# Loads of x in chunks of ten tokens paced by transposes, with masks built first, in a fused convolution and expert kernel

## Chip, core and metric

The kernel runs on one NeuronCore of a Trainium2 chip. The metric is the device time of one execution in microseconds; the time before is the median of three runs.

## What is computed

Inputs are `x` (8 batches x 4160 tokens x 192 channels, float32), `weight_gen` (8 x 4160 x 8 heads x 7 taps) and the weights of a small expert network. First a dynamic convolution: every token has its own softmax over seven taps per head, and the output is the weighted sum of the token and its six predecessors. Then a mixture of depths: a gate scores every output row, the 128 highest rows of each batch go through two matrix products, and the result, scaled by a sigmoid of the score, is added to these rows.

```python
w = softmax(weight_gen, axis=-1)                       # (B, S, H, K)
out = einsum('bshk,bskhg->bshg', w, windows(x, K))     # causal, zero padded, K = 7
scores = einsum('bsd,d->bs', out, w_gate)
for b in range(B):
    top = argpartition(-scores[b], 128)[:128]
    y = maximum(out[b, top] @ w1, 0) @ w2              # 192 -> 1024 -> 192
    out[b, top] += sigmoid(scores[b, top])[:, None] * y
```

## The kernel before

The 33,280 rows are laid on 128 partitions of 260 consecutive tokens each (`SP = 260`). `phase()` (L584) holds all the work of interest. Its main loop (L873) makes 65 passes, `NSUB = 65`, each for four tokens of every partition (`C = 4`). The code is under `manual_schedule`, so each engine executes its instructions in the order in which the program writes them; only dependencies make an engine wait.

`x` lives in a ring `xr` of 168 tokens (`RING`) and six of padding, in float16. `load_x(a, b)` (L599) brings in tokens a to b of all partitions; it is issued on POOL's queue and converts from float32. A slot of the ring can be overwritten once the products and transposes that read it are done.

In one pass of the loop:

- VectorE multiplies a window of x by the weights: `products` (L769, instruction at L781), into one of three `prod` buffers.
- TensorE adds the seven taps of the pass before with 28 small matmuls: `tap_sums` (L785, L791), into `cps`. ScalarE copies that out to `co` (L799), one of three buffers, and SP's queue stores it in two halves (L801).
- ScalarE and TensorE do the softmax of later weights in pieces of four passes: `exps` (L627, L630), `sums` (L644), `scaled` (L648). Weight pieces come by `load_wg` (L613) on SP's queue, three pieces ahead. `dup_weights` (L759) doubles a piece for the products.
- `dots()` (L674) computes each token's dot products with the gate. Its work is cut into groups of eight 128-wide transposes of x (L711), 5.33 tokens, that ScalarE copies to `xT` (L715) and TensorE multiplies by `gmat` (L696). `DOTS = 0.66` lets 1.32 groups run in each pass, so the dots run ahead of the products. A few passes later `score()` (L719) turns them into scores, and when all are known the selection and the expert passes follow.

Loads of x follow three rules. Tokens 0 to 12 are loaded at the start. The thirteen chunks between the entries of `edges` (L835: 12, 24, 34, 44, 54, 64, 76, 90, 104, 118, 132, 146, 160, 168) are each tied to the exponentials of weight piece 1 to 13 (L636 to L643): POOL issues the load once that ScalarE instruction has run. The tokens after 168 come in chunks of 20 at passes worked out in `late` (L860), without such a tie.

`gate_matrix()` (L111) and `selection_masks()` (L125) are small selects and ramps on POOL. The first needs `wcol`, four tiny loads by `load_gate()` (L104) on SP's queue. `expert_weights()` (L176) clears two tiles and loads `w1` and `w2` from POOL. The order of the start of `phase()` is written out in L817 to L858.

Of the kernel before, what the change touches and what calls it, by code (L numbers as in the profile page):

```python
# [20 lines left out]
def kernel(  # L21
# [10 lines left out]
    nc = tc.nc  # L32
    B, S, D = x.shape
# [4 lines left out]
    PAD = K - 1  # L38
    P = 128
    N = B * S  # L40
    SP = N // P
# [3 lines left out]
    RING = 168  # L45
    C = 4
# [5 lines left out]
    RUN = 128  # L52
    GRP = 8
# [530 lines left out]
    def phase():  # L584
# [23 lines left out]

        pieces = [(0, 1), (1, 3), (3, 5)] + [(a, a + 4) for a in range(5, NSUB, 4)]
# [17 lines left out]
        def exps(n):  # L627
            m = pieces[n][1] - pieces[n][0]
            es[n] = ep.tile([P, m, K, CH], FP16, tag="e", name="e")
            begun = nc.scalar.activation(  # L630
                out=es[n][:, :, :, :],
                in_=wgts[n].rearrange("p (s c) h k -> p s k (c h)", c=C), func=AF.Exp
            )
            if n + 3 < NP:
                load_wg(n + 3)
            if n in paced:  # L636
                tc.add_manual_dep(
                    load_x(*paced[n]).ins, begun.ins.name,
                    mybir.DependencyInfo(
                        mybir.DependencyClass.Sync, mybir.DependencyReason.DATA  # L640
                    ), reason="x chunks follow the weight pieces",
                )
# [31 lines left out]
        def dots():  # L674
# [7 lines left out]
            for i in range(len(plan) + 2):  # L682
# [20 lines left out]
                if i < len(plan):  # L703
# [11 lines left out]
                    nc.scalar.copy(out=xT[:, 0:m, :], in_=tps[:, 0:m, :])  # L715
                    xTs[i] = xT
                yield
# [100 lines left out]
        load_wg(0)  # L818
        make_identity(nc, identity[:])
# [13 lines left out]
        load_gate()  # L833
        load_wg(2)
        edges = [12, 24, 34, 44, 54, 64, 76, 90, 104, 118, 132, 146, 160, RING]  # L835
        paced = dict(enumerate(zip(edges[:-1], edges[1:]), 1))
# [19 lines left out]
        gate_matrix()  # L856
        selection_masks()
        sm = softmax()  # L858

        late = []  # L860
        for a in range(RING, SP, 20):
            b = min(SP, a + 20)
            free = (b - RING + PAD - 1) // C + 1
            late.append((max(free, int((a + PAD) / (2 * DOTS * RUN * GRP / D)) - 4), a, b))
# [8 lines left out]
        for g in range(NSUB + 1):  # L873
# [34 lines left out]
            if late and g >= late[0][0]:  # L908
                load_x(*late.pop(0)[1:])
            if g == 10:  # L910
                selection_constants()
            if g == 34:
                expert_weights()
# [9 lines left out]
    DOTS = 0.66  # L923
    with ExitStack() as cctx:
        with tc.manual_schedule():
            phase()
# [84 lines left out]
```

## Time and profile before

| what | value |
|---|---|
| time, median of 3 runs | 327.6 us (327.27 to 327.63) |
| the profiled execution | 326.92 us |
| its span in the profile | 325.2 us |
| VectorE (DVE) busy | 249.1 us, 77% |
| TensorE (PE) busy | 195.0 us, 60% |
| ScalarE (ACT) busy | 188.7 us, 58% |
| GpSimd (POOL) busy | 59.3 us, 18% |
| mean DMA rate | 158 GB/s |

The profile is of one execution, taken by the hardware profiler; its times count from the span's start. The busy shares are means over stages that differ: loading and convolving at first, then the end of the convolution beside the selection, then the expert passes. Queues are named after the engine that issues: SPq, POOLq. "Idle before, releaser" names what ended an engine's wait; a wait for several things is put down to the last.

### The profile page before, as it was taken

Reading aid. Unit: us, or ns where it says so; the run is one execution under the profiler, and the core shown is the slowest. Engines: PE = TensorE matmul, PEld = TensorE weight load, DVE = VectorE, ACT = ScalarE, POOL = GpSimd, SP = SyncE. Lnnn points to the kernel's source line nnn. Section 1 sums busy time; section 2 is a strip of 40 time slices with the busy share of each in tenths; the row PEclk is TensorE's granted clock in tenths of the full one; section 3 lists DMA queues with packets and bytes.
Section 4 is the critical chain, followed back from the end, with each engine's and each line's share of the span. In section 5 each row is a group of like instructions: output and inputs, shape, how many; then the busy total and the mean of one; then the engine's idle time right before and its main releaser. Section 6 shows DMA issues by size and latency. Waiting matters only on the chain.

```text
span 325.2 us, 7474 instructions
## 1 busy us (share of the span) xinstructions
PE 195.0 (60%) x3177; PEld 124.2 (38%) x3177; DVE 249.1 (77%) x249; ACT 188.7 (58%) x282; POOL 59.3 (18%) x81
## 2 busy tenths in 40 slices
PE   0287569796979150979887563133735777678300
PEld 0255336464647030656554222011513444455200
DVE  3789559999999380499999999999997778884000
ACT  4699299999999224799975512001432657555200
POOL 2880000000030400000000000000327852000180
PEclk9999559979997875699998965555585799999855
DMA  7959989999989999545563543011377986333320
GB/s 165 296 174 227 273 220 235 248 243 263 261 236 225 232 233 271 120 120 143 152 149 97 147 108 88 1 48 48 73 171 128 188 166 132 100 73 93 83 80 21
DMA packets 28080, 51.48 MB, mean 158 GB/s; under 512 B 4805, under 2 KB 22219, under 8 KB 28042
## 3 DMA queue, kind: packets, MB, share of 16 engines
q1 hardware_dynamic: 21962, 33.62, 35.1%
q0 software_dynamic: 6080, 17.34, 29.5%
q8 instruction: 26, 0.43, 0.5%
q14 instruction: 12, 0.10, 0.1%
HBM read 41.60 MB, written 26.35 MB: 209 GB/s over the span
## 4 chain that ended last, share of the span: by engine, by line
DVE 31%; PE 22%; ACT 16%; DMA 16%; issue 9%; POOL 3%; SPq 1%; POOLq 0%; ACTq 0%; DVEq 0%
DVE prod L781 20%; DMA out_dram<-co 13%; PE cps L791 10%; ACT e L630 4%; ACT co L799 4%; PE tps L711 4%; ACT xT L715 2%; POOL out_dram L417 2%; PE den L189 2%; PE yps L696 2%; ACT wd L762 2%; DMA wg_t<-in_weight_gen_dram 2%; DVE above L492 1%; PE sps L740 1%; DVE cnt L498 1%
## 5 line engine op out<-in xcount | busy, mean ns | idle before, releaser
L781 DVE TENSOR_TENSOR prod<-xr,wd 128x5376 f16<-128x5376 f16 (+1 forms) x84 | 192.3, 2315 | 5.7 <-PE cps L791 3.2
L791 PE MATMUL cps<-prod,ident 64*64 64x384 f16 x1820 | 112.7, 378 | 11.3 <-DVE prod L781 10.6
L799 ACT COPY co<-cps 128x768 f32<-128x768 f32 x65 | 52.6, 809 | 66.3 <-PE cps L791 33.6
L791 PEld LDWEIGHTS <-ident 64*64 64x64 f16 x1820 | 50.4, 119 | 63.5 <-issue 26.8
L715 ACT COPY xT<-tps 128x1024 f16<-128x1024 f16 (+1 forms) x50 | 50.7, 1022 | 5.3 <-PE tps L711 5.0
L249 POOL DMA_INDIRECT wsel<-in_weight_gen_dram,row_i x8 | 11.7, 1462 | 124.2 <-DVE win_i L217 122.0
L711 PE MATMUL tps<-ident,xr 128*128 128x128 f16 x399 | 34.0, 235 | 0.0
L630 ACT ACTIVATE e<-wg_t 128x896 f16<-128x896 f32 (+2 forms) x18 | 29.9, 1661 | 3.1 <-DMA wg_t<-in_weight_gen_dram 3.1
L696 PE MATMUL yps<-gmat,xT 128*128 128x8 f16 (+1 forms) x399 | 17.9, 169 | 20.4 <-ACT y L701 18.8
L762 ACT COPY wd<-w 128x1792 f16<-128x1792 f16 (+2 forms) x18 | 28.0, 1553 | 0.8 <-DVE w L650 0.8
L696 PEld LDWEIGHTS <-xT 128*128 128x128 f16 x399 | 14.4, 98 | 34.9 <-issue 29.5
L711 PEld LDWEIGHTS <-xr 128*128 128x128 f16 x399 | 25.7, 105 | 0.6 <-issue 0.6
L601 POOL DMA_DIRECT2D xr<-in_x_dram x20 | 10.9, 552 | 82.0 <-ACT e L630 38.1
L189 PEld LDWEIGHTS <-ident 128*128 128x128 f16 x182 | 10.7, 105 | 38.5 <-issue 35.5
L189 PE MATMUL den<-e,ident 128*128 128x128 f16 (+2 forms) x126 | 11.2, 238 | 18.6 <-ACT e L630 14.5
L733 DVE TENSOR_TENSOR sp<-w,y 128x1792 f16<-128x1792 f16 (+2 forms) x9 | 8.9, 990 | 13.5 <-ACT y L701 13.5
L740 PE MATMUL sps<-sp,ident 128*128 128x256 f16 (+2 forms) x63 | 8.4, 278 | 14.8 <-ACT lnd L197 12.9
L417 POOL DMA_INDIRECT out_dram<-xr,row_i x8 | 7.8, 978 | 37.6 <-issue 37.6
L320 DVE TENSOR_TENSOR xr<-xr,wes 128x1344 f16<-128x1344 f16 x8 | 6.9, 858 | 8.4 <-ACT wes L314 6.5
L369 ACT ACTIVATE hT<-hps 128x512 bf16<-128x512 f32 x16 | 9.5, 601 | 5.2 <-PE hps L365 5.2
L740 PEld LDWEIGHTS <-ident 128*128 128x128 f16 x63 | 5.8, 102 | 17.0 <-issue 16.0
L271 POOL DMA_INDIRECT xr<-in_x_dram,win_i x8 | 11.1, 1390 | 5.9 <-DVE xr L320 4.1
(126 smaller groups left out, 173.5 us busy)
## 6 DMA issues: line engine op xcount, KB each, us to landing
out_dram<-co SPq DMA_DIRECT2D x130, 192.0 KB, 3.4
wg_t<-in_weight_gen_dram SPq DMA_DIRECT2D x15, 448.0 KB, 5.6
xr<-in_x_dram POOLq DMA_DIRECT2D x6, 672.0 KB, 8.8
xr<-in_x_dram POOLq DMA_DIRECT2D x4, 960.0 KB, 17.3
xr<-in_x_dram POOLq DMA_DIRECT2D x4, 480.0 KB, 5.8
xr<-in_x_dram POOLq DMA_DIRECT2D x3, 576.0 KB, 9.7
xr<-in_x_dram POOLq DMA_DIRECT2D x2, 384.0 KB, 7.2
halo<-in_x_dram SPq DMA_DIRECT2D x1, 504.0 KB, 5.2
```

The costliest lines, as they stand in the source:

```text
L189: nc.tensor.matmul(out=den[:, :, :], lhsT=ident16[:, :], rhs=e_k(k), start=(k == 0), stop=(k == K - 1),)
L249: nc.gpsimd.indirect_dma_start(out=wsel[:, b, :], out_offset=None, in_=wg_flat[:, :], in_offset=bass.IndirectOffsetOnAxis(ap=row_i[:, b:b ...
L417: ins = nc.gpsimd.indirect_dma_start(out=out_flat[:, :], out_offset=bass.IndirectOffsetOnAxis(ap=result["at"][:, b:b + 1], axis=0), in_=re ...
L630: begun = nc.scalar.activation(out=es[n][:, :, :, :], in_=wgts[n].rearrange("p (s c) h k -> p s k (c h)", c=C), func=AF.Exp)
L696: nc.tensor.matmul(out=o, lhsT=lhs, rhs=m, start=(w == 0), stop=(w == 2), skip_group_check=True,)
L711: nc.tensor.transpose(out=tps[:, j, :], in_=xflat[:, e0:e0 + RUN], identity=ident16[:, :],)
L715: nc.scalar.copy(out=xT[:, 0:m, :], in_=tps[:, 0:m, :])
L740: nc.tensor.matmul(out=sps[:, :, :], lhsT=ident16[:, :], rhs=sp[:, :, k, :], start=(k == 0), stop=(k == K - 1),)
L762: nc.scalar.copy(out=wd[:, 0:b - a, :, :, :], in_=w16[:, a:b, :, :, None].to_broadcast([P, b - a, K, CH, 2]),)
L781: nc.vector.tensor_tensor(out=pv[:, k0:k1], in0=xwin[:, k0:k1], in1=wv[:, k0:k1], op=MUL)
L791: nc.tensor.matmul(out=cps[64 * j:64 * j + 64, i, 0:HB], lhsT=ident16[rows, rows], rhs=pf[rows, k, j * HB:(j + 1) * HB], start=(k == 0), s ...
L799: nc.scalar.copy(out=co[:, :, :], in_=cps[:, :, 0:HB])
```

## The change

All loads of x after token 12 now come from one list. Two chunks of 12 tokens are tied to the exponentials of weight pieces 1 and 2. All others, of ten tokens (two of two tokens, where the ring or the row ends), are tied to ScalarE's copy of a transpose group: a chunk is released by the first group i for which its first token, plus the padding of six, lies at or before the end of what group i + 6 begins with (`LEAD = 6`). `load_gate()` is called before the halo loads, `gate_matrix()` and `selection_masks()` before the third weight load and the first products, and `expert_weights()` at pass 46 instead of 34.

```diff
+        STEP = 10
+        chunks = [(12, 24), (24, 36)]
+        while chunks[-1][1] < SP:
+            a = chunks[-1][1]
+            chunks.append((a, min(SP, a + STEP, RING if a < RING else SP)))
+
+        def next_chunk(begun):
+            tc.add_manual_dep(
+                load_x(*chunks.pop(0)).ins, begun.ins.name,
+                mybir.DependencyInfo(mybir.DependencyClass.Sync, mybir.DependencyReason.DATA),
+                reason="x chunks are loaded at the pace of the gate dots",
+            )
...
-            if n in paced:
-                tc.add_manual_dep(
-                    load_x(*paced[n]).ins, begun.ins.name,
...
-                )
+            if n in (1, 2):
+                next_chunk(begun)
...
-                    nc.scalar.copy(out=xT[:, 0:m, :], in_=tps[:, 0:m, :])
+                    begun = nc.scalar.copy(out=xT[:, 0:m, :], in_=tps[:, 0:m, :])
                     xTs[i] = xT
+                    while chunks and chunks[0][0] + PAD <= (i + LEAD) * RUN * GRP // D:
+                        next_chunk(begun)
...
         load_x(0, 4)
         load_wg(0)
+        load_gate()
         make_identity(nc, identity[:])
...
         load_wg(1)
         load_x(4, 12)
-        load_gate()
+        gate_matrix()
+        selection_masks()
         load_wg(2)
-        edges = [12, 24, 34, 44, 54, 64, 76, 90, 104, 118, 132, 146, 160, RING]
-        paced = dict(enumerate(zip(edges[:-1], edges[1:]), 1))
...
-        gate_matrix()
-        selection_masks()
         sm = softmax()
...
-            if late and g >= late[0][0]:
-                load_x(*late.pop(0)[1:])
             if g == 10:
                 selection_constants()
-            if g == 34:
+            if g == 46:
                 expert_weights()
...
+    LEAD = 6
```

POOL's order at the start of the program, as a difference (a load of 128x2304 is 12 tokens; `gsel` and `gmat` belong to the gate matrix):

```order
 L601 DMA xr<-in_x_dram 128x1536
-L601 DMA xr<-in_x_dram 128x2304
 L114 AFFINE_SELECT gsel<-wcol 128x8
 L119 AFFINE_SELECT gmat<-gsel 128x8
```

The load of tokens 12 to 24 leaves its place ahead of the selects; it now follows all of them and the masks.

POOL's order behind the last ramp of the masks, the same difference (1920 is ten tokens, 2688 fourteen, 3840 twenty, 384 two; `w_b` is the first instruction of the expert weights):

```order
-L601 DMA xr<-in_x_dram 128x1920 x4
-L601 DMA xr<-in_x_dram 128x2304
-L601 DMA xr<-in_x_dram 128x2688 x6
-L601 DMA xr<-in_x_dram 128x1536
-L601 DMA xr<-in_x_dram 128x3840 x4
-L601 DMA xr<-in_x_dram 128x2304
...
+L601 DMA xr<-in_x_dram 128x2304 x2
+L601 DMA xr<-in_x_dram 128x1920 x13
+L601 DMA xr<-in_x_dram 128x384
+L601 DMA xr<-in_x_dram 128x1920 x9
+L601 DMA xr<-in_x_dram 128x384
 L177 MEMSET w_b 64x1024
```

Seventeen loads become twenty-six, of ten tokens but for four, and the expert weights stand directly behind the last of them in both kernels.

SP's order at its start, the same difference:

```order
-L616 DMA wg_t<-in_weight_gen_dram 128x224
-L824 DMA halo<-in_x_dram 15x1152
-L824 DMA halo<-in_x_dram 112x1152
-L616 DMA wg_t<-in_weight_gen_dram 128x448
+L629 DMA wg_t<-in_weight_gen_dram 128x224
 L106 DMA wcol<-in_moe_w_gate_dram 128x1
 L107 DMA wcol<-in_moe_w_gate_dram 64x1
 L108 DMA wcol<-in_moe_w_gate_dram 64x1
 L109 DMA wcol<-in_moe_w_gate_dram 128x1
...
+L835 DMA halo<-in_x_dram 15x1152
+L835 DMA halo<-in_x_dram 112x1152
+L629 DMA wg_t<-in_weight_gen_dram 128x448 x2
```

The four loads of `wcol` pass the two halo loads and the second weight piece.

## Rows read from the trace of the kernel before

**Rows 1.** Busy share of the DMA engines in 40 slices of the page.

```profile
DMA  7959989999989999545563543011377986333320
```

**Rows 2.** Engines by stretch: stretch, length, busy us of each, PEclk, DMA share, GB/s.

```profile
24.00:44.00 20.00, 11.27 (x201) 7.82 (x199) 12.87 (x8) 13.04 (x18) 0.64 (x2) 0.72 1.01 250
44.00:75.00 31.00, 28.25 (x486) 18.46 (x484) 29.40 (x27) 29.87 (x38) 2.01 (x4) 0.85 0.98 232
75.00:105.00 30.00, 24.56 (x455) 16.57 (x455) 29.46 (x16) 29.41 (x37) 3.71 (x7) 0.94 0.99 251
105.00:135.00 30.00, 11.69 (x157) 7.17 (x158) 11.41 (x8) 11.88 (x16) 3.70 (x7) 0.66 1.00 230
135.00:155.00 20.00, 17.72 (x361) 12.10 (x353) 19.95 (x11) 19.59 (x25) 0.00 (x0) 0.99 0.47 121
```

**Rows 3.** Timeline of DVE: start us, us, instruction [idle before, releaser].

```profile
43.85 0.74 DVE L733 TENSOR_TENSOR sp<-w,y 128x1120 f16<-128x1120 f16 x1 [7.13 <-ACT y L701]
...
115.03 1.09 DVE L733 TENSOR_TENSOR sp<-w,y 128x1792 f16<-128x1792 f16 x1 [6.41 <-ACT y L701]
...
131.91 0.42 DVE L751 TENSOR_REDUCE scores<-ss 128x32 f32<-128x256 f32 x1 [9.52 <-ACT ss L745]
135.05 5.83 DVE L781 TENSOR_TENSOR prod<-xr,wd 128x5376 f16<-128x5376 f16 x2 [2.71 <-PE cps L791]
...
145.20 2.95 DVE L781 TENSOR_TENSOR prod<-xr,wd 128x5376 f16<-128x5376 f16 x1
...
152.34 5.81 DVE L781 TENSOR_TENSOR prod<-xr,wd 128x5376 f16<-128x5376 f16 x2
```

**Rows 4.** Waits in 24 to 44 us, then in 105 to 135 us: total, times, longest.

```profile
ACT co L799 <- DMA out_dram<-co: 6.9, 2, 4.8
...
ACT co L799 <- DMA out_dram<-co: 15.9, 3, 5.9
```

**Rows 5.** Chain that ended last: start us, us, what.

```profile
104.02 24.48 DMA out_dram<-co
```

**Rows 6.** Timeline of POOL.

```profile
8.87 0.53 POOL L601 DMA_DIRECT2D xr<-in_x_dram  x1 [5.65 <-ACT e L630]
9.40 0.20 POOL L114 TENSOR_SCALAR_AFFINE_SELECT gsel<-wcol 128x8 f32<-128x8 f32 x1
...
10.22 2.83 POOL L114 TENSOR_SCALAR_AFFINE_SELECT gsel<-wcol 128x8 f32<-128x8 f32 x1 [0.35 <-DMA wcol<-in_moe_w_gate_dram]
...
21.49 2.15 POOL L601 DMA_DIRECT2D xr<-in_x_dram  x4
...
94.96 2.65 POOL L601 DMA_DIRECT2D xr<-in_x_dram  x5 [10.07 <-ACT e L630]
...
107.33 0.53 POOL L180 DMA_DIRECT2D w_a<-in_moe_w_dram  x1
```

**Rows 7.** Loads of x issued in 20:24, 44:94 and 94:106 us, to landing.

```profile
DMA to landing us min/median/max: 5.8/5.8/5.8
...
DMA to landing us min/median/max: 7.7/8.8/10.7
...
DMA to landing us min/median/max: 10.2/19.6/24.2
```

**Rows 8.** Queues: q0 in 24:27 and 106:122 us, q1 in the whole span.

```profile
q0 software_dynamic: 170, 0.59, 102.2%
...
q0 software_dynamic: 462, 2.96, 88.8%
...
q1 hardware_dynamic: 21962, 33.62, 35.1%
```

**Rows 9.** Start: SP's first wcol load and its third weight load, ACT's second exponential.

```profile
2.63 0.43 SPq L106 DMA_DIRECT2D wcol<-in_moe_w_gate_dram  x1
...
5.05 16.83 SPq L616 DMA_DIRECT2D wg_t<-in_weight_gen_dram  x7
...
7.56 1.01 ACT L630 ACTIVATE e<-wg_t 128x448 f16<-128x448 f32 x1 [2.17 <-DMA wg_t<-in_weight_gen_dram]
```

More of the change, by code (lines that the diff above doesn't have):

```diff
@@ L635, in exps @@
                 load_wg(n + 3)
-            if n in paced:
-                tc.add_manual_dep(
-                    load_x(*paced[n]).ins, begun.ins.name,
-                    mybir.DependencyInfo(
-                        mybir.DependencyClass.Sync, mybir.DependencyReason.DATA
-                    ), reason="x chunks follow the weight pieces",
-                )
+            if n in (1, 2):
+                next_chunk(begun)
         def sums(n):
@@ L855, in phase @@
                 )
-        gate_matrix()
-        selection_masks()
         sm = softmax()
[L860 to L864, printed above, removed]
         dt, sc, sel = dots(), score(), None
```

## Prediction

> **What bounds the kernel now.** I read the 40 slices of the page first, then the five engines by stretch, then DVE's timeline wherever its busy time fell, then who waited there, and last the queues that lay behind it.
>
> The slices [rows 1] show the DMA engines at nine tenths or more from about 24 to 130 us and at about half afterwards: all of x is brought in during the first 40% of the span. By stretch [rows 2], DVE and ACT are both almost full from 44 to 105 us (DVE 29.40 of 31.00 us, then 29.46 of 30.00), and DVE is full again from 135 us. In 24 to 44 us DVE works 12.87 of 20 us and in 105 to 135 us 11.41 of 30. In those two stretches DMA is at 1.00, so they are what a change of loads can touch.
>
> DVE's timeline [rows 3] has the holes one by one: 7.13 us before the instruction at 43.85, then 6.41, 9.52 and 2.71 us before those at 115.03, 131.91 and 135.05. Sum: **25.8 us**. The named releasers are ACT copies, but ACT itself waits there [rows 4]: its copy out of `cps` waits 6.9 us and 15.9 us for `out_dram<-co`, that is, for a store to free one of three `co` buffers. ACT runs its list in order, so everything queued behind that copy (the `xT`, `y`, `ss` copies, the exponentials) waits too, and DVE and PE with it. One such store took 24.48 us [rows 5].
>
> Why the stores were late stands in POOL's timeline [rows 6]: four x loads in one burst at 21.49 us, and five at 94.96, four of those of 20 tokens. Loads that DMA has in hand together land 10.2 to 24.2 us after issue, against 5.8 for a chunk of 10 tokens that lands first and 7.7 to 10.7 for 14 tokens issued singly [rows 7]. Each burst goes out just before a hole.
>
> **The price of a byte.** A token is 128 x 192 x 2 = 49,152 bytes as written, so x is 12.78 MB. On the queue of x [rows 8], 0.59 MB of 10-token chunks took 102.2% of 3 us, 5.2 us per MB; mostly 20-token chunks took 88.8% of 16 us for 2.96 MB, 4.8 per MB. The queue of stores and weights took 35.1% of 325.2 us for 33.62 MB, 3.4 per MB. One store step (4 tokens, 0.393 MB) is then 1.34 us of all 16 engines, a weight piece (0.459 MB) 1.56, a chunk of 10 tokens 2.6.
>
> **The change, part by part.** I call one pass of the loop over g a step; there are 65.
>
> *Chunks tied to transpose groups.* In the order before, pacing went by weight pieces and by g; now 10 tokens go out about every 1.9 groups (5.33 tokens each). The dots run 1.32 groups a step, so this is 7.0 tokens a step, and the last load goes out near step 34. No two full chunks go out together after the first few. Where the bursts were, a store now finds at most a chunk or two ahead. Both holes should close: **-25.8 us**, bounds -25.8 and 0 (nothing closes).
>
> *What is late next.* The bytes stay, so I add up DMA for one step of the new pace: x 7.0 x 0.0492 MB x 5.2 = 1.79 us, store 1.34, weights 0.69 (softmax runs at 4/3 weight steps a group, four to a piece: 0.44 pieces x 1.56); sum 3.8 us. DVE without x loads takes 3.46 us a step: two products at 135.05, three single ones (that at 145.20 is one) and the next at 152.34 [rows 3], so five steps in 17.29 us. Checking the price at 44 to 105 us: the stores of 17 steps, 7 weight pieces, 6 chunks of 14 tokens and about 28 tokens of the burst make 22.8 + 10.9 + 21.5 + 6.6 = 61.8 us, where DMA was busy 60 of 61; so the sum is some 3% high and a step needs 3.7. From step 8 to step 34 that is up to 26 x 0.25 = 6.5 us over DVE's pace. Against it stand a lag of two steps that three `co` buffers allow (2.7 us) and the chunks already issued but not yet due. Bounds 0 and 6.5; I take **+4**, nearer the upper end, since DMA at 0.98 to 0.99 in 44 to 105 us [rows 2] is the nearest row and shows little slack.
>
> *Start.* SP now issues the four `wcol` loads before the halo and the second weight piece. They took from 2.63 to 5.05 us [rows 9], so both leave 2.4 us later. ACT waited 2.17 us for that piece, until 7.56, and the first product hangs on it. Bounds 0 (x would use the engines meanwhile, and the sum of bytes until then is the same) and +2.4; I take the middle, **+1.2**.
>
> *Masks ahead.* The selects move from behind the load of tokens 12 to 24 to before it. POOL's select at 10.22 lasted 2.83 us beside a product of DVE, where the ones before it took 0.2 [rows 6]. `wcol` is asked for 1.3 us earlier, behind a single weight load, so I expect selects and masks to be done before the first product, at 0, and the two loads behind them to go out as soon as the exponentials allow, the second some 8 us earlier than in the burst at 21.49. Bounds: 0, and the price of the fourth rival below.
>
> *Expert weights.* g from 34 to 46 moves nothing on POOL: no other POOL instruction lies between, and they still follow the last x load, as at 107.33 [rows 6]. They come later only because that load does. 768 KB at x's price is 4.1 us of DMA, now beside a DMA share of 0.47 [rows 2]: nothing. If that cover were gone it would be 4 us.
>
> *More DMAs.* 28 loads of x for 20, each 0.53 us of a POOL that waits anyway: nothing. The Trainium skill (DMA: Bandwidth & Descriptors, "Bandwidth") advises batches of 1 MiB or more, with about 2 us fixed for each DMA; by that rule eight more would cost up to 16 us and the sum below would be near 323. The rows disagree: chunks of 10 tokens kept the engines at 102% and cost 5.2 against 4.8 us per MB, so the fixed part overlaps, and the small surcharge is in the sum above.
>
> After step 34 nothing changes in any engine's order: the 170 us behind 155 us stay.
>
> **Sum.** -25.8 + 4 + 1.2 = -20.6 us. The profiled execution took 326.9 us (span 325.2), 0.7 under the median of 327.6. From the median: **307.0 us**.
>
> **The rivals.**
> 1. *DMA becomes the bound.* The bursts are spread, but every step needs 3.8 us of DMA and no lag helps: 26 x 0.35 = 9.1 us, plus the full 2.4 at the start: 327.6 - 25.8 + 11.5 = 313.3. For it: DMA at 1.00. Against: DVE is nearly full beside it.
> 2. *Nothing is given back.* The DMA sum is too high, and the start costs nothing: 327.6 - 25.8 = 301.8. For it: DVE at 29.46 of 30 us beside the old loads. Against: DMA at 0.99 in the same row.
> 3. *The lead is too short, and it gets slower.* A chunk must land in the time of five groups, 5 x 3.46 / 1.32 = 13.1 us; later, each chunk stalls PE's transposes, and ACT and DVE behind them. If landings were 19.6 us, the median around the second burst [rows 7], the same five groups would take 19.6 us: 5.2 us a step, 1.7 over DVE's, 26 x 1.7 = 44 us, so 327.6 - 25.8 + 1.2 + 44 = 347. It costs from 13.1 us on and decides from about 16.7 us, where 26 steps lose the 24.6 gained. Against: 10.7 was the longest of those issued singly, with more tokens. The Trainium skill (SBUF — State Buffer, "SBUF: two separate sides") names such a mechanism, descriptors of a POOL-issued DMA that cannot be written while DVE holds the shared port. The trace does not bear it out: loads issued beside products landed in 7.7 to 10.7 us.
> 4. *The masks block the early load.* If `wcol` lands after about 8 us, the selects meet the products as at 10.22, and tokens 12 to 24 go out near 21.5 instead of 8.87, landing 5.8 later at 27.3, where product 3 stood at 21.2: 307.0 + 6.1 = 313.1.
>
> **How the numbers follow.** Forecast 0.60, rivals 0.18, 0.10, 0.05, 0.07. The range runs from rival 2 with a microsecond to spare to rivals 1 and 4 with one or two: 300.5 to 315. A difference of 0.2% (0.65 us) is about what a measurement can tell from no change; all but rival 3 lie far below it. Faster 0.94, same 0.01, slower 0.05.
>
> **What would show it.** Right: no ACT wait for `out_dram<-co` above a microsecond; DVE near 3.5 us a step from the first product on, step 34 starting near 135 us instead of 155; DMA at 0.9 or more until then with no landing of x over 13 us; the first product near 11 us. Wrong: PE waiting in front of transposes for x (rival 3); POOL selects of 2.8 us in the first 20 us (rival 4); DVE holes spread over 40 to 135 us with DMA at 1.00 (rival 1); or holes of the old size anywhere.

## The result, and the profile after

| | change | before | ratio, 95% interval |
|---|---|---|---|
| median of 4 runs each, us | 315.97 | 327.62 | 0.9638 (0.9561 to 0.9715) |
| lowest to highest, us | 314.31 to 318.39 | 327.27 to 329.61 | |
| profiled execution, us | 314.31, span 312.6 | 326.9, span 325.2 | |

The change gains 11.65 us where 20.6 were forecast, and the time lies 1.0 us above the range.

The 40 slices of the page after the change, DMA's busy share in tenths, beside [rows 1]:

```profile
DMA  7797999999999997999996331112467986233220
```

Nine tenths reach to 164 us now (slices of 7.8 us; one of 7 at 117 to 125), and the half-busy stretch behind 130 us is gone. The five engines by stretch after the change (columns and order as in [rows 2]):

```profile
24.00:44.00 20.00, 17.68 (x313) 11.93 (x315) 18.77 (x10) 19.79 (x25) 1.58 (x3) 0.91 0.89 220
44.00:75.00 31.00, 25.43 (x427) 16.43 (x430) 26.80 (x26) 26.65 (x36) 3.17 (x6) 0.83 0.99 239
75.00:105.00 30.00, 24.08 (x423) 15.54 (x419) 27.67 (x16) 28.32 (x36) 2.90 (x6) 0.89 0.99 246
105.00:135.00 30.00, 24.15 (x431) 16.13 (x424) 27.61 (x16) 26.13 (x33) 3.23 (x7) 0.88 0.95 221
135.00:155.00 20.00, 16.80 (x300) 10.76 (x298) 18.19 (x9) 16.78 (x22) 4.99 (x10) 0.91 0.99 214
```

DVE, the third pair, rises from 12.87 to 18.77 us and from 11.41 to 27.61 us where the holes were. But it falls from 29.40 to 26.80, from 29.46 to 27.67 and from 19.95 to 18.19 in the stretches that were full. The waits of the copy out of `cps` in the whole span (total, times, longest), before:

```profile
ACT co L799 <- DMA out_dram<-co: 22.8, 5, 5.9
```

and after, where ten added lines make it L809:

```profile
ACT co L809 <- DMA out_dram<-co: 4.1, 6, 1.5
```

So the long waits of [rows 4] are gone, as forecast; the longest left is 1.5 us, where the prediction named a microsecond as the sign of being right. DVE's timeline after the change, beside [rows 3]:

```profile
12.11 0.82 DVE L862 TENSOR_SCALAR xr<-halo,keep_p 128x1152 f16<-128x1152 f32 x1 [7.36 <-DMA halo<-in_x_dram]
14.96 5.82 DVE L791 TENSOR_TENSOR prod<-xr,wd 128x5376 f16<-128x5376 f16 x2
...
42.31 2.95 DVE L791 TENSOR_TENSOR prod<-xr,wd 128x5376 f16<-128x5376 f16 x1
...
52.59 2.96 DVE L791 TENSOR_TENSOR prod<-xr,wd 128x5376 f16<-128x5376 f16 x1 [2.31 <-PE cps L801]
...
79.53 2.96 DVE L791 TENSOR_TENSOR prod<-xr,wd 128x5376 f16<-128x5376 f16 x1 [0.77 <-ACT wd L772]
...
87.56 5.83 DVE L791 TENSOR_TENSOR prod<-xr,wd 128x5376 f16<-128x5376 f16 x2 [1.34 <-PE cps L801]
...
153.03 2.96 DVE L791 TENSOR_TENSOR prod<-xr,wd 128x5376 f16<-128x5376 f16 x1 [1.72 <-ACT ss L755]
```

The largest hole between 40 and 155 us is 2.31 us, where it was 9.52. In place of four large holes there are many small ones.

**The account.** The start of a step's product on DVE dates the step. Step 0 starts at 14.96 us (before: 10.04), step 8 at 42.31 (44.51), step 34 at 141.61 (155.20). Steps 8 to 34 take 99.30 us, 3.82 us each. Before, they took 110.69 us, 18.64 of it in the holes at 115.03, 131.91 and 135.05 [rows 3], and 3.54 us each without these. So against the profiled execution before, step 34 stands at -25.77 (the four holes) + 4.92 (the start) + 7.25 (99.30 less 92.05) = -13.60 us. Another 1.0 is lost behind step 34, and -12.6 is what the spans differ by. The profiled execution, 314.31 us, is the shortest of the four; in e11, the same kernel profiled at 316.53 us, steps 8 to 34 take 100.69 us, 8.64 more than 92.05.

**The start.** DMA in 4 to 6 and in 6 to 8 us (columns of [rows 2]), before:

```profile
4.00:6.00 2.00, 0.00 (x0) 0.00 (x0) 0.59 (x4) 0.99 (x3) 0.00 (x0) 1.00 1.04 300
6.00:8.00 2.00, 0.00 (x0) 0.00 (x0) 0.82 (x1) 0.44 (x1) 0.00 (x0) 1.00 0.90 198
```

and after:

```profile
4.00:6.00 2.00, 0.00 (x0) 0.00 (x0) 0.59 (x4) 0.97 (x3) 0.00 (x0) 1.00 0.99 132
6.00:8.00 2.00, 0.00 (x0) 0.00 (x0) 0.00 (x0) 0.00 (x0) 0.06 (x1) 1.00 0.98 131
```

The engines are about as busy, and move less than half as much, then two thirds. The second weight piece is in the chain of work after the change (start, us, what); ACT's exponential behind it follows from ACT's timeline:

```profile
4.52 7.93 DMA wg_t<-in_weight_gen_dram
...
12.48 1.01 ACT L643 ACTIVATE e<-wg_t 128x448 f16<-128x448 f32 x1 [7.13 <-DMA wg_t<-in_weight_gen_dram]
```

The piece is asked for 2.35 us later than at 2.17, and takes 7.93 us to land. The exponential starts 4.92 us later than in [rows 9], and so does the first product.

**The loads of x.** POOL after the change, beside [rows 6]:

```profile
8.34 0.20 POOL L114 TENSOR_SCALAR_AFFINE_SELECT gsel<-wcol 128x8 f32<-128x8 f32 x1
...
11.77 1.20 POOL L146 IOTA ramp<- 128x167 int32 x5
13.78 0.55 POOL L601 DMA_DIRECT2D xr<-in_x_dram  x1 [0.81 <-ACT e L643]
...
140.61 0.53 POOL L601 DMA_DIRECT2D xr<-in_x_dram  x1 [5.40 <-ACT xT L723]
...
148.16 0.53 POOL L601 DMA_DIRECT2D xr<-in_x_dram  x1 [3.16 <-ACT xT L723]
148.73 0.95 POOL L177 MEMSET w_b<- 64x1024 bf16 x1
```

and the time from issue to landing of the loads from 28 us on, beside [rows 7]:

```profile
DMA to landing us min/median/max: 4.9/7.8/9.4
```

No burst is left, selects take 0.2 us, and no load takes longer than 9.4 us. One of them was late all the same, that of 140.61, the last but one of ten tokens. This is PE's wait for it:

```profile
150.03 0.29 PE L719 MATMUL tps<-ident,xr 128*128 128x128 f16 x1 [2.42 <-DMA xr<-in_x_dram]
```

### The profile page after: what moved, and what is told of

Same layout as the page of the kernel before. It is cut to its first block, busy times and chain, and to the rows that moved or that the text cites. A ratio compares the mean times of both kernels' runs of the same rounds, so it can differ in the third digit from the quotient of the medians.

```text
span 312.6 us, 7490 instructions
## 1 busy us (share of the span) xinstructions
PE 194.0 (62%) x3177; PEld 123.2 (39%) x3177; DVE 249.6 (80%) x249; ACT 188.9 (60%) x282; POOL 56.5 (18%) x89
## 3 DMA queue, kind: packets, MB, share of 16 engines
q0 software_dynamic: 7232, 17.34, 35.1%
## 4 chain that ended last, share of the span: by engine, by line
DVE 27%; ACT 23%; PE 18%; DMA 17%; issue 8%; POOL 3%; SPq 2%; POOLq 0%; ACTq 0%; DVEq 0%
DVE prod L791 16%; DMA out_dram<-co 14%; PE cps L801 8%; ACT co L809 6%; ACT xT L723 5%; ACT e L643 4%; PE tps L719 3%; ACT wd L772 3%; DMA wg_t<-in_weight_gen_dram 3%; POOL out_dram L417 2%; PE den L189 2%; DVE above L492 1%; PE yps L704 1%; DVE cnt L498 1%; PE sps L750 1%
## 5 line engine op out<-in xcount | busy, mean ns | idle before, releaser
L809 ACT COPY co<-cps 128x768 f32<-128x768 f32 x65 | 52.5, 808 | 47.8 <-PE cps L801 33.0
L601 POOL DMA_DIRECT2D xr<-in_x_dram x28 | 15.1, 539 | 122.8 <-ACT xT L723 103.4
L189 PEld LDWEIGHTS <-ident 128*128 128x128 f16 x182 | 10.6, 104 | 43.3 <-issue 40.3
L719 PEld LDWEIGHTS <-xr 128*128 128x128 f16 x399 | 25.8, 105 | 2.9 <-DMA xr<-in_x_dram 2.6
L249 POOL DMA_INDIRECT wsel<-in_weight_gen_dram,row_i x8 | 10.3, 1288 | 70.0 <-DVE win_i L217 67.9
L271 POOL DMA_INDIRECT xr<-in_x_dram,win_i x8 | 14.0, 1754 | 3.7 <-DVE xr L320 1.6
L501 PE MATMUL tot<-cnt,block 128*128 128x23 f16 x4 | 0.7, 178 | 19.1 <-DVE cnt L498 19.1
L658 DVE TENSOR_TENSOR w<-e,r 128x896 f16<-128x896 f16 (+2 forms) x18 | 10.3, 572 | 2.2 <-ACT r L199 2.1
```

The lines of the kernel that those rows point to most:

```text
L189: nc.tensor.matmul(out=den[:, :, :], lhsT=ident16[:, :], rhs=e_k(k), start=(k == 0), stop=(k == K - 1),)
L271: nc.gpsimd.indirect_dma_start(out=win_of(b), out_offset=None, in_=x_elems, in_offset=bass.IndirectOffsetOnAxis(ap=win_i[:, b:b + 1], axis=0),
L601: return nc.gpsimd.dma_start(out=xr[:, o:o + b - a, :], in_=bass.AP(tensor=x_flat.tensor, offset=x_flat.offset + a * D, ap=[[SP * D, P], [ ...
L719: nc.tensor.transpose(out=tps[:, j, :], in_=xflat[:, e0:e0 + RUN], identity=ident16[:, :],)
L809: nc.scalar.copy(out=co[:, :, :], in_=cps[:, :, 0:HB])
```

## The experiments

**Step starts of all kernels**, from one profile each; times are medians of 4 runs (e2: 10), ratios each against the kernel before on the same chip. e1 to e4 shared a chip (before: 328.06 us), e5 to e8 (327.24), e9 to e12 (325.31), e13 to e15 (326.20).

| kernel | step 0 | step 8 | step 34 | us a step, 8 to 34 | time, us | ratio (95%) |
|---|---|---|---|---|---|---|
| change | 14.96 | 42.31 | 141.61 | 3.82 | 315.97 | 0.964 (0.956 to 0.972) |
| e11, change again | 14.73 | 42.43 | 143.12 | 3.87 | 316.85 | 0.970 (0.961 to 0.979) |
| e1, old start | 10.16 | 37.58 | 140.42 | 3.96 | 313.84 | 0.953 (0.944 to 0.963) |
| e2, start alone | 15.00 | 42.94 | 155.70 | - | 326.45 | 0.996 (0.992 to 1.001) |
| e3, half the stores | 15.45 | 43.22 | 137.94 | 3.64 | 306.02 | 0.934 (0.928 to 0.940) |
| e4, lead 10 | 15.00 | 46.13 | 144.12 | 3.77 | 317.31 | 0.971 (0.964 to 0.978) |
| e5, e1 and e3 | 10.28 | 37.60 | 134.06 | 3.71 | 304.39 | 0.931 (0.924 to 0.939) |
| e6, no stores to step 35 | 15.42 | 42.92 | 139.68 | 3.72 | 310.12 | 0.949 (0.940 to 0.957) |
| e7, four `co` | 15.44 | 42.76 | 139.64 | 3.73 | 312.00 | 0.956 (0.948 to 0.963) |
| e8, new start | 9.97 | 38.28 | 140.75 | 3.94 | 311.65 | 0.957 (0.947 to 0.968) |
| e9, half the copy | 14.71 | 41.95 | 139.58 | 3.76 | 307.81 | 0.941 (0.932 to 0.949) |
| e12, e6 and e9 | 15.32 | 42.55 | 131.74 | 3.43 | 301.03 | 0.923 (0.917 to 0.930) |
| e10, e7 and e8 | 9.88 | 38.20 | 134.56 | 3.71 | 305.20 | 0.934 (0.926 to 0.942) |
| e15, e10 again | 9.88 | 38.71 | 133.77 | 3.66 | 306.44 | 0.939 (0.934 to 0.945) |
| e13, chunks of 20 | 15.29 | 42.62 | 143.69 | 3.89 | 313.88 | 0.959 (0.952 to 0.966) |
| e14, e10 and chunks of 20 | 9.78 | 38.49 | 136.48 | 3.77 | 307.17 | 0.940 (0.932 to 0.949) |

The change and e10 were each profiled twice: their pace differs by 0.05 us a step between takes. That is the least by which one profile can be off: the runs of one kernel differ by up to 4 us and more, and the profiled one was the longest in e1, e6 (308.76 to 312.44) and e9 (304.59 to 308.72), and the shortest in the change. So the medians are read beside the steps below. e3, with half the stores, has a faster pace (3.64) than e6 with none (3.72); no run explains that, and a difference of this size is not to be taken for an effect.

### e1 to e4: which part of the change, which limit

e1 keeps the pacing and undoes the start. Edit, against the change:

```
-        load_gate()
...
-        gate_matrix()
-        selection_masks()
+        load_gate()
...
+        gate_matrix()
+        selection_masks()
```

(The first three lines stand ahead of the halo and behind `load_x(4, 12)`; now the loads of `wcol` follow `load_x(4, 12)`, and the masks the loop over the first pieces.)

> The changed kernel with the start of the kernel before: the gate loads behind the second weight piece, gate matrix and masks behind the first two products. Theory S (the start alone costs what the first product lost, 14.96 against 10.04 us, because the 384 tiny wcol packets delay the halo and the second weight piece): first product near 10.0 us, time 311 us, 4.9 under the change's 316.0. Rival S2 (the lost start is absorbed: DMA is full until about 150 us, so an earlier start only moves DMA's backlog): first product near 10 us but step 34 at 141 to 142 us as in the change, time 315 to 316. Rival M (masks behind the products hold back tokens 24 to 36, which go out near 21.5 us): a hole of 2 to 5 us before step 6 to 9, time 312 to 316.

Measured: the first product is back at 10.16 us and step 8 starts 4.73 us ahead of the change, but step 34 only 1.19 ahead: 3.96 us a step. 313.84 us, and its interval overlaps that of the change. Its profiled run, 316.09 us, was the longest of its four, so these step dates show it at its worst and e8 is the better witness for an earlier start.

e2 has the start alone, on the kernel before:

```
+        load_gate()
         make_identity(nc, identity[:])
...
-        load_gate()
+        gate_matrix()
+        selection_masks()
...
-        gate_matrix()
-        selection_masks()
```

> The kernel before with only its start changed: gate loads ahead of the halo, gate matrix and masks ahead of the third weight load. Theory S: first product near 15 us and the whole time 4.9 us longer, 332.5 us. Rival S2 (absorbed by the hole of 7 us before step 8, which is set by DMA's burst): first product near 15 us, step 8 still at 44 to 45 us, time 327 to 329. With the masks gone from its way the burst could also start earlier and shrink the hole: then under 327.

Measured: the first product comes at 15.00 us as in the change, and the whole takes 326.45 us against 328.06, no longer. The hole of 7.13 us before step 8 [rows 3] takes the loss in:

```profile
42.28 0.74 DVE L733 TENSOR_TENSOR sp<-w,y 128x1120 f16<-128x1120 f16 x1 [0.17 <-ACT y L701]
42.94 2.95 DVE L781 TENSOR_TENSOR prod<-xr,wd 128x5376 f16<-128x5376 f16 x1
```

So the start by itself moves 4.9 us, and has no price as long as a later stage makes everyone wait anyway.

e3 stores half of the convolution's output:

```
-            for j in range(2):
+            for j in range(1):
```

> The changed kernel with only the first of the two half stores of every step, so half of the convolution's output is not written. DMA work of a step falls by 0.67 us, nothing else changes on DVE, ACT or PE. Theory A (between step 8 and step 34 a step costs its bytes on 16 full DMA engines, 3.82 us): steps fall to DVE's pace of about 3.46 to 3.5 us, step 34 starts 8 to 9 us earlier than 141.6 us, time near 307. Rival B (the in-order engines hold each other up at that pace whatever DMA does): steps stay at 3.8 us, step 34 within 2 us of 141.6, time 314 to 316.

Measured: 3.64 us a step and 306.02 us. Step 34 comes 3.67 us earlier than in the change, and behind step 34, where stores are halved too, it takes 166.58 us in place of 170.99. The stores weigh on steps 8 to 34; whether by their bytes or by what waits for them, e6 and e7 tell.

e4 asks for each chunk ten groups ahead:

```
-    LEAD = 6
+    LEAD = 10
```

> The changed kernel with the chunks released ten groups ahead instead of six, same bytes, same chunk size. Theory A (DMA throughput): steps 8 to 34 at the same 3.8 us, step 34 within 2 us of 141.6 us, time 314 to 317. Rival L (the chunks land too late, PE's transposes wait for them and the rest queues behind): steps near 3.5 us, step 34 6 to 9 us earlier, time 307 to 310.

Measured: 317.31 us. The hole before step 8 is back in part (3.80 us, step 8 at 46.13), behind two chunks that go out together at 27.66 and 28.17 us, and landings are 6.3 to 8.2 us. A longer lead does not help the middle; the late chunk at the end does not occur with it, and behind step 34 it takes 170.1 us (before 170.0, the change 171.0).

### e5 to e8: bytes, buffers, and a start without the loss

e5 joins the edits of e1 and e3:

```
-            for j in range(2):
+            for j in range(1):
...
-        load_gate()
...
+        load_gate()
...
+        gate_matrix()
+        selection_masks()
```

> Old start with the new pacing, as in the run with the pacing alone, and only the first half store of every step, so half of the convolution's output is not written. Theory A (DMA's backlog swallowed the 4.8 us that the old start is ahead by at the first product; with half the store bytes there is no backlog to swallow it): first product near 10 us, step 34 near 133 us against 137.9 with the new start, time 301 to 302. Rival C (the in-order engines fall into the same delays whenever they run that close): step 34 within 2 us of 137.9, time 305 to 306.

Measured: 304.39 us and step 34 at 134.06, 3.88 us ahead of e3's 137.94, of 5.17 at step 0. With fewer stores three quarters of the gain at the start reach step 34; in e1's one profile, of its longest run, it was a quarter. Of this, 1.5 us are left at the end of the span (303.0 and 304.5), and the ratios, 0.931 and 0.934, do not tell the two apart.

e6 issues no store for steps 0 to 35:

```
-            for j in range(2):
+            for j in range(0 if s < 36 else 2):
```

> The changed kernel without the stores of steps 0 to 35, so that part of the output is not written. DMA need of a step falls from 3.8 to about 2.5 us, far under DVE's 3.46. Theory A alone (the bytes are all that held steps over DVE's pace): steps 8 to 34 at 3.46 us, step 34 near 133 to 134 us, with the first product still at 15 us. Theory A with C (the half stores run still lost 0.2 us a step to waits among PE, ACT and DVE themselves): steps at 3.6 us, step 34 at 136 to 138 us. Time 303 to 306 in either.

Measured, by stretch (columns of [rows 2]):

```profile
44.00:75.00 31.00, 25.63 (x452) 16.86 (x450) 28.20 (x26) 28.67 (x36) 3.17 (x6) 0.89 0.75 153
75.00:105.00 30.00, 24.91 (x431) 16.15 (x434) 27.93 (x16) 28.32 (x36) 3.17 (x6) 0.89 0.66 143
```

DMA falls from 0.99 to 0.75 and 0.66, and a step takes 3.72 us, in the longest of its four runs; the median, 310.12 us, is 5.9 under the change's. So the stores are part of what holds these steps, but DMA's bytes are not all of it, and the first rival, which has them alone, falls. What is left, in 40 to 141 us, are waits for ACT and for PE behind it:

```profile
PE sps L750 <- ACT lnd L197: 6.0, 4, 2.5
...
DVE prod L791 <- PE cps L801: 4.3, 5, 1.7
```

e7 gives the copies a fourth buffer, and takes its room from the ring of x:

```
-    RING = 168
+    RING = 160
...
-        outp = cctx.enter_context(tc.tile_pool(name="outp", bufs=3))
+        outp = cctx.enter_context(tc.tile_pool(name="outp", bufs=4))
```

> The changed kernel with four co buffers instead of three, for which the ring is cut from 168 to 160 tokens. Theory A (bytes): step 34 within 1.5 us of 141.6 us, time 314 to 317. Rival B (single late stores, of up to 12 us, hold ACT's copies now and then and the loss is not made up): ACT's 3.0 us of waits for stores go, step 34 3 to 5 us earlier, time 311 to 313.

Measured: 3.73 us a step and 312.00 us, with all stores. In 37 to 145 us one copy waits for a store, 0.3 us. By the medians this is 4.0 of the 5.9 us that e6 gains, though e7's interval still overlaps that of the change: most of what the stores cost here is the wait for a buffer. That DMA's bytes have no part in it is not shown, since 3.73 is also what the prediction's sum of bytes gives (3.7 to 3.8).

e8 asks for `wcol` behind the halo, the second weight piece and `load_x(4, 12)`, still builds the masks ahead of the first product, and puts the matrix that needs `wcol` behind it:

```
-        load_gate()
...
-        gate_matrix()
+        load_gate()
         selection_masks()
...
                     advance(sm)
+                if g == 0 and half == 0:
+                    gate_matrix()
```

> The changed kernel with another start: gate loads behind the halo and the second weight piece, masks (which need no load) first on POOL, then the two chunks of 12 tokens, then the gate matrix. First product near 10 us as before the change, tokens 12 to 24 out near 9 us and 24 to 36 near 12.5 us instead of 21.6 as in the run with the pacing alone. Theory A (bytes; DMA idles 2 to 4 us less in the first 24 us): step 34 at 137 to 139 us, time 311 to 313. Rival S2 (any start is absorbed): step 34 at 140 to 142 us, time 314 to 316.

Measured on DVE:

```profile
7.04 0.82 DVE L861 TENSOR_SCALAR xr<-halo,keep_p 128x1152 f16<-128x1152 f32 x1 [2.22 <-DMA halo<-in_x_dram]
...
9.97 5.82 DVE L791 TENSOR_TENSOR prod<-xr,wd 128x5376 f16<-128x5376 f16 x2
```

So it was the place of `wcol`'s loads ahead of halo and weights, not the masks, that cost the start. Yet of 4.0 us ahead at step 8 only 0.9 are left at step 34 (2.4 of 4.2 against e11): copies wait 5.4 us for stores in 37 to 145 us, in the change 3.0. So part of the gain runs into the three buffers; how much is not settled, since the medians, 311.65 against 315.97 and 316.85, differ by 4.3 and 5.2 us, with intervals that overlap.

### e9 to e12: ACT, both limits at once, and a better kernel

e9 lets ACT copy half of `cps` and store that half twice, so that the stores keep their bytes:

```
-            nc.scalar.copy(out=co[:, :, :], in_=cps[:, :, 0:HB])
+            nc.scalar.copy(out=co[:, 0, :], in_=cps[:, 0, 0:HB])
...
-                    in_=co[64 * j:64 * j + 64, :, :],
+                    in_=co[64 * j:64 * j + 64, 0:1, :].to_broadcast([64, 2, HB]),
```

> The changed kernel with ScalarE's copy of the tap sums cut to half its width (768 to 384 columns), and both halves of the store reading that half, so that the bytes stored are the same and half of the output is not the convolution. Nothing changes on DMA, DVE or PE; ACT has some 0.3 us less to do in each step. Theory C2 (without stores a step still took 3.72 us, so the floor is ACT, which is as full as DVE while the exponentials run, 3.47 us of work a step, and whose backlog makes PE idle and lose its clock): steps 8 to 34 fall from 3.82 to 3.5 to 3.6 us, step 34 near 134 to 137 us, time 307 to 311. Theory A (bytes): 3.8 us, step 34 within 1.5 us of 141.6, time 314 to 316.

Measured: 3.76 us a step in place of 3.82 and 3.87, in the longest of its four runs. ACT is busy 81.45 us in steps 8 to 34 in place of 89.37; much of the time saved is spent waiting for stores (37 to 145 us; the change in its two takes: 3.0 and 2.3):

```profile
ACT co L809 <- DMA out_dram<-co: 12.1, 9, 3.2
```

The total, 307.81 us, is 9.0 under e11 on the same chip, but 4.3 of that come behind step 34 (167.4 us against 171.7 in e11), where the copy is shorter as well.

e12 joins e6 and e9:

```
-            nc.scalar.copy(out=co[:, :, :], in_=cps[:, :, 0:HB])
-            for j in range(2):
+            nc.scalar.copy(out=co[:, 0, :], in_=cps[:, 0, 0:HB])
+            for j in range(0 if s < 36 else 2):
```

> The half-width copy together with no stores in steps 0 to 35, so part of the output is not written: both suspects relieved. Theory C2 (ACT is the floor, DMA through late stores the rest): steps 8 to 34 at 3.45 to 3.55 us, step 34 near 133 to 135 us with the first product at 15 us. If something else holds the steps (PE's order or its clock): 3.65 us or more, step 34 at 138 us or later.

Measured, by stretch:

```profile
44.00:75.00 31.00, 24.70 (x489) 16.69 (x487) 31.00 (x28) 29.82 (x43) 3.70 (x7) 1.00 0.80 169
75.00:105.00 30.00, 26.02 (x484) 17.14 (x484) 30.00 (x18) 28.15 (x40) 3.70 (x7) 0.96 0.77 152
```

DVE is busy 31.00 of 31 and 30.00 of 30 us, and a step takes 3.43. Of the kernels tried only this one, with both relieved, runs at DVE's pace. By the profiles, against the change's 3.82 to 3.87, e6 alone gains 0.10 to 0.15 us a step, e9 alone 0.06 to 0.11, both together 0.39 to 0.44. That they gain more together than singly is not shown: e6 and e9 were profiled in their longest runs. By the medians against e11, less what each gains behind step 34, e6 has 6.1 us, e9 4.8 and e12 11.5, which about add up.

Two rivals stay untested. e12 takes away the stores' bytes together with the wait for buffers; half the copy with four buffers and all stores was not run, so whether all bytes fit at DVE's pace is not known. The change moves 235 GB/s over steps 8 to 34; at 3.43 us a step the same bytes would need some 262, an estimate from its 99.30 us. For one stretch that was reached, in e15, with DVE almost full (75 to 105 us, columns of [rows 2]):

```profile
75.00:105.00 30.00, 22.44 (x436) 15.18 (x434) 29.65 (x17) 29.67 (x38) 3.72 (x7) 0.98 1.04 269
```

And half the copy frees `cps` sooner as well as ACT, and PE's granted clock is 1.00 and 0.96 in e12's two stretches, 0.83 and 0.89 in the change; which of these the steps gain by was not tried apart.

e10 joins e7 and e8 and computes everything:

```
-    RING = 168
+    RING = 160
...
-        outp = cctx.enter_context(tc.tile_pool(name="outp", bufs=3))
+        outp = cctx.enter_context(tc.tile_pool(name="outp", bufs=4))
...
-        load_gate()
...
-        gate_matrix()
+        load_gate()
...
+                if g == 0 and half == 0:
+                    gate_matrix()
```

> The changed kernel with the new start (gate loads behind the second weight piece, masks first, gate matrix after the chunks of 12 tokens) and four co buffers with a ring of 160 tokens. Each alone gave 312. If the start's gain was lost only to stores held in three buffers: first product near 10 us, steps 8 to 34 at 3.73 us, step 34 near 135 to 136 us, time 307 to 308. If DMA's backlog takes it even so: steps at 3.85 us or more, step 34 near 138 to 139 us, time 310 to 311.

Measured: 305.20 us, 11.65 under e11 on the same chip. Step 0 is 4.85 us ahead of e11, step 34 8.56: with the fourth buffer the early start is kept, and more is gained on top. Singly, by the medians, e7 and e8 stand 4.9 and 5.2 us under e11. e11 is the change again, for a second profile beside e9, e10 and e12:

> The change itself once more, on the same chip as the other three of this group, as their measure: time 314 to 317, step 34 between 141 and 144 us. No theory differs on it.

Measured: 316.85 us. In 40 to 141 us DVE waits 5.0 us for PE's tap sums (the change 5.5) and ACT 2.3 for stores (2.6), within 0.5 us of the change, but DVE waits 2.0 us for `wd` (0.8), and PE waits once for x, 1.5 us.

### e13 to e15: the number of loads

e13 asks for x in chunks of 20 (16 loads in place of 28, counting the two of the start; the expectation's 14 leaves these out), e14 does so on e10, e15 is e10 again:

```
-        STEP = 10
+        STEP = 20
```

> The changed kernel with chunks of 20 tokens instead of ten, same lead of the first token: 14 loads of x instead of 28. Theory F (each DMA has a fixed cost on the 16 engines; the queue of x took 109.7 us for the 17.34 MB that took 95.9 before): the queue falls to 92 to 98 us, steps 8 to 34 get some 0.05 to 0.15 us shorter, time 312 to 314. Rival T (a chunk of 20 tokens holds the stores up twice as long at a time and lands later, against three co buffers and the same lead): ACT's waits for stores rise from 4 us to 8 us or more, time 318 to 324.

> The kernel with the new start and four co buffers, with chunks of 20 tokens. Theory F: the queue of x falls by some 12 us, but stores no longer hold ACT in this kernel (0.4 us), so the time is unchanged within 1.5 us of 305. Rival T: stores held up again, PE waits for late chunks, 308 to 312.

> The kernel with the new start and four co buffers once more, as the measure of the other two on this chip: 303 to 307, steps 8 to 34 at 3.7 us.

Measured: the queue of x over the whole span (packets, MB, share of 16 engines' span), before:

```profile
q0 software_dynamic: 6080, 17.34, 29.5%
```

the change:

```profile
q0 software_dynamic: 7232, 17.34, 35.1%
```

and e13:

```profile
q0 software_dynamic: 5504, 17.34, 33.0%
```

For the same bytes the queue takes 95.9, 109.7 and 103.1 us (share times spans of 325.2, 312.6 and 312.5). Half of the change's surplus goes with the twelve loads, (109.7 - 103.1) / 12 = 0.55 us each. The rest stays, though e13 has fewer loads (16) than the kernel before (20), so the number of loads alone does not set the queue's time. Theory F put the queue at 92 to 98 us. Rival T's sign is there in part: copies wait 6.6 us for stores in 37 to 145 us, in the change 3.0 and 2.3. The times tell nothing apart: e13 is 313.88 against 315.97 and 316.85 for the change, with overlapping intervals, e14 307.17 (304.82 to 309.33) against 306.44 (306.24 to 306.70) for e15. The number of loads has no price here that these runs can show.

## Why the prediction was wrong, step by step

**Right: the holes, -25.8.** They closed entirely, for the reason given: no burst, and no store of long duration behind one (24 to 155 us: 12.4 us at most, where one took 24.48). The longest wait for a store fell from 5.9 to 1.5 us. DMA at 0.89 to 0.99 up to 155 us and landings up to 9.4 us were also as forecast.

**Failed: "What is late next", +4, measured +7.25, above its own bound of 6.5.** The step held DVE's pace against a sum of DMA's bytes and found DMA alone in the way; ACT, named as almost full beside DVE, does not enter it, and the three `co` buffers only as a cushion of 2.7 us. DVE's pace was read rightly: 3.46 us a step, and e12 runs at 3.43. But taking it as the pace that the kernel keeps was wrong. It came from 135 to 152 us, where DMA's share was 0.47 and where, in ACT's timeline before the change, only one exponential stands, as against seven in the 61 us of 44 to 105:

```profile
141.09 1.80 ACT L630 ACTIVATE e<-wg_t 128x896 f16<-128x896 f32 x1
```

ACT's load stood in [rows 2]: busy 29.87 of 31 and 29.41 of 30 us, and there steps 8 to 25 took 61.16 us, 3.60 each. In the stretch of DVE's pace too ACT was busy 19.59 of 20 us. In the change it works 89.37 us in steps 8 to 34, 3.44 a step, so that DVE's pace leaves it no slack. The sum also took +4 over DVE's 3.46, but subtracted the holes from a time whose 26 steps already stood at 3.54 without them: 26 x 0.08 = 2.1 us are counted twice, and without this slip the forecast would have been 304.9, further off. And ACT and the stores meet: a copy that waits 1 us for a buffer makes a full, in-order ACT late by 1 us for all that is queued behind it. e6, e7 and e9 show that both count, by 5.9, 4.0 and 8.2 us of the medians (3.6 of e9's behind step 34), and in e12, with both relieved, DVE has no wait left in these steps. In the change DVE idles 8.9 us from 44 to 135 us (31 - 26.80, 30 - 27.67, 30 - 27.61), and DVE's waits in 40 to 141 us all name PE or ACT: 5.5 us for PE's tap sums to free a `prod`, 2.4 for `ss`, 0.8 for `wd`.

One of them link by link, from the timeline of all engines around 44 to 53 us:

```profile
44.00 1.73 ACT L772 COPY wd<-w 128x1792 f16<-128x1792 f16 x1
...
45.59 1.06 ACT L723 COPY xT<-tps 128x1024 f16<-128x1024 f16 x1
...
46.70 0.80 ACT L809 COPY co<-cps 128x768 f32<-128x768 f32 x1
...
47.40 0.28 ACT L197 ACTIVATE lnd<-den 128x128 f32<-128x128 f32 x1
...
47.73 1.09 PE L750 MATMUL sps<-sp,ident 128*128 128x160 f16 x7 [2.62 <-ACT lnd L197]
...
52.59 2.96 DVE L791 TENSOR_TENSOR prod<-xr,wd 128x5376 f16<-128x5376 f16 x1 [2.31 <-PE cps L801]
```

The softmax sums in `den` were done at 45.11, but ACT reaches `lnd` only at 47.40, behind three copies. The score sums of PE (`sps`) want the PSUM buffer that `lnd` frees, so PE stands for 2.62 us. Then this stretch follows (columns of [rows 2]):

```profile
47.50:52.60 5.10, 4.87 (x56) 2.81 (x55) 1.55 (x3) 3.42 (x7) 0.00 (x0) 0.50 1.02 223
```

PE works 4.87 of 5.10 us at a granted clock of 0.50, the level of 1.2 GHz, after it had idled; its tap sums come late, and DVE waits 2.31 us for a `prod`. The Trainium skill (TensorE: Matmul & The Clock Gate, "Part 1: The HAM clock gate") says that the reduced clock is the default and that activity lifts it; the 0.50 behind the idle time agrees. A 2.6 us delay on ACT is thus handed on once by PE's standing still and again by its slower work. That this chain is behind most of the 8.9 us is argued from the named waits, not shown: it was not tried with a `den` of its own, and in e12, where DVE has no wait in steps 8 to 34, PE still waits 4.0 us for `lnd` in 37 to 145 us.

**Failed: "Start", +1.2, measured +4.92, above its bound of 2.4.** The bound held that a load passed by others leaves 2.4 us later and lands as much later. It did leave 2.35 later, but it took 7.93 us in place of 5.37 from issue to landing, beside DMA that was busy and moved 131 GB/s in place of 198 to 300. What it costs in the total hangs on what comes after: nothing in e2 (the hole took it); with the old start 0.9 us at step 34 in e8 and 1.2 in e1 come back (three buffers take in the rest), 5.1 in e10 against e7, and 3.9 in e5 against e3.

**Not clear of noise: "After step 34 nothing changes", 0, measured +1.0.** The same kernel takes 171.0 and 171.7 us there (the change and e11), or 169.0 and 170.8 (e10 and e15). One thing did change, and two sentences of the prediction meet in it. Rival 3 asked that a chunk land within five groups, put at 13.1 us. The chunk asked for at 140.61 was wanted 7.0 us later, when PE came to stand at 147.61, because the groups came faster by then, with copies to `xT` 1.9 us apart from 139.28 to 146.82 where the 13.1 has 2.6; it landed after 9.4 us. Steps 36 to 38 take 7.88 us where they took 6.07 before; the other 0.8 of the difference is regained later. e4, with ten groups ahead, has no such wait and takes 6.07 us there. But e6 and e7, with six groups ahead, take 6.07 as well, and behind step 34 they need 171.1 and 170.9 us, so it is not shown that the wait is what costs the 1.0. Rival 3's mechanism was there, singly (in e11 also at 97.20 us), not 26 times.

**Right in the rest.** Masks: all selects 0.2 us, done at 12.97, ahead of the first product; rival 4 did not come. The two loads behind them left at 13.78 and 17.22 us, the second 4.3 us earlier than in the burst and not 8, since the exponentials that release them came 4.9 us later. Expert weights: directly behind the last x load, as said, though under a DMA share of 0.99 (135 to 155 us) where a share of 0.47 had been named as their cover; what that costs was not tried apart. More loads: the price in DMA time was mis-sized, 13.8 us more of the queue where the text's 5.2 against 4.8 us per MB makes some 5; a price in time these runs do not show. The Trainium skill (DMA: Bandwidth & Descriptors, "Anatomy of one DMA — SWDGE (gpsimd) path") puts the fixed part of a DMA at some 2 us; as an estimate from that figure, 12 fewer loads would be worth up to 24 us. They saved 0.55 us each of queue time and no time that can be told.

**Rivals.** The first gave 313.3, the nearest time, with a cause that is not enough: e6 takes a quarter to a third of DMA's work away, and 3.72 us a step remain. The second (301.8) lies near e12's 301.03 us, where the stores and half of ACT's copy are taken away, but in part by chance: e12 has the late start, and its shorter copy gains 3.6 us behind step 34 (167.39 us).

**The sum again**, from 307.0: +3.25 (late next), +3.7 (start), +1.0 (behind step 34) make 315.0; the median is 315.97. The terms are not independent: with the start of before, in e8, steps 8 to 34 take 102.47 us in place of 99.30.

**What stays open.** What slows the packets in 4 to 8 us was not isolated: e8 shows that `wcol`'s place decides, not how. In the kernel before, the last of the same loads were still outstanding at 8 to 10 us beside 251 GB/s:

```profile
8.00:10.00 2.00, 0.53 (x7) 0.42 (x7) 0.27 (x1) 1.05 (x3) 0.92 (x3) 1.00 1.05 251
```

## What to carry to other kernels

When a stall of one resource is removed, work out the load of a step for every engine and not only for the one that looks longest: here ACT, with 3.44 us beside DVE's 3.46, was the second limit, and it was missing in the sum. Where two resources lie close to the same pace, and one waits for buffers that the other frees, test them singly and together: here each relief gained some us, and only both brought DVE's pace. Read the medians beside the steps of one profile, since by the profiles alone the two seemed to gain only together. A gain at the start counts only as far as no later wait takes it in: in e2 a late start cost nothing, and a better start and one more buffer (e10) were worth 11.65 us together.

## What the runs showed of the hardware

- Four loads of `wcol`, of 512 bytes at most, ahead of the halo and the weights cost the first product 4.9 us, not the 2.4 us that they took to issue: the large one behind took 7.93 us in place of 5.37, while DMA was 0.98 to 0.99 busy at 131 to 132 GB/s.
- The same 17.34 MB took the queue of x 95.9, 103.1 or 109.7 us, by how they were cut and when they were sent; a busy share of DMA of 0.99 is therefore no proof that bytes are the limit. From 75 to 105 us the change moves 246 GB/s at a share of 0.99 and e15 269 at 1.04.
- PE's granted clock stood at 0.50 for 5 us behind an idle time of 2.62 us, in the midst of a stretch with a mean of 0.83.
